# Queries and selection of the last twelve pairs as rows, turned into the score operand by one DMA transpose per head

## The chip, the cores and the metric

The kernel runs on one core of a Trainium2 chip. The metric is device microseconds of one execution; the figure for a kernel is the median of several runs. Work is done by TensorE (PE in the profile; PEld are its weight loads), VectorE (DVE), ScalarE (ACT) and GpSimd (POOL). SyncE (SP) computes nothing: it issues DMAs, in the order of its queue, and a DMA that has to wait for a semaphore holds up what stands behind it. Sixteen DMA engines serve all queues.

## The reference

The program is sparse attention followed by a feed-forward block. There are 4 batches, 8 heads, 768 positions and head dimension 64. Keys are cut into 24 chunks of 32. For each query an upper bound of the score is formed for every chunk from the chunk's smallest and largest key, and the 6 best causal chunks are kept:

```python
k_min, k_max = k_chunks.min(axis=3), k_chunks.max(axis=3)
ub = np.sum(np.maximum(q[:, :, :, None, :] * k_min[:, :, None, :, :], q[:, :, :, None, :] * k_max[:, :, None, :, :]), axis=-1)
ub = np.where(causal, ub, -1e9)
top_chunks = np.argsort(ub, axis=-1)[..., -6:]
scores = np.where(sel & causal_mask, scale * q @ k.T, -1e9)
attn = softmax(scores) @ v
```

The eight heads of a position are then one row of 512. Each row is divided by its root mean square and multiplied by a gain, and goes through `(silu(x @ w_gate) * (x @ w_val)) @ w_out` with a hidden width of 1536.

## The kernel before

**Pairs.** Two heads of one batch are a pair, since 2 x 64 dimensions fill 128 partitions. There are 16 pairs, 0 to 15, four for each batch, numbered in order of the batches.

**Preparation of a pair (`prep`).** The two heads' keys and queries are loaded in fp32 as rows, positions on partitions (`knat`, `qnat`; two DMAs each on SP's queue, line 479). TensorE turns them with six fp32 transposes each (line 498), and ScalarE or VectorE evicts them to `kt` and `qt`, dimensions on partitions. From `kt`, VectorE reduces the chunks' maxima and minima; from `qt` and its positive part `rt`, TensorE forms the bounds `ub` (line 586), which are turned back so that positions are on partitions (`up`), masked (`ubm`, line 618) and searched by twelve MAX8 instructions (line 631). `pick` (line 639 and 644) compares the bounds of both heads with their sixth best in one instruction and writes, beside the comparison, one column with a guard value from the best bound. Its destination is `selq`: 128 positions x 6 blocks x 2 heads x 64 columns.

**The score operands.** For each head of a pair there are two bf16 tiles of 128 partitions x 768 positions. `ke` holds 64 rows of keys and the rows of `e_all`, a constant with a large negative number where a key's chunk is. `qs` holds 64 rows of queries and the rows of the selection, so that one matmul gives the score and the penalty for chunks that aren't selected. Head 0 has the queries in partitions 0 to 63 and the selection in 64 to 127, head 1 the other way round. The query half is cast from `qt` (step qC: GpSimd, line 298; for pair 0 GpSimd or ScalarE). The selection half takes a step selT, six bf16 transposes of `selq` on TensorE into the PSUM tile `st` (line 655), and a step selC, two evictions `qs<-st` by ScalarE or VectorE. Three sets of operands exist, so three pairs can be in flight.

**Scores, product, norm.** `scores` computes key block by query block (`sc`, line 718), ScalarE exponentiates into `pt` (line 735), GpSimd masks the diagonal blocks for batches 1 to 3 (line 741), TensorE multiplies with the values `vx` (`av`, line 754; `vx` is loaded and cast by a DMA on GpSimd's queue, line 456), and VectorE divides into `xb`. `norm` scales the rows to `xs`; they are turned into `xT` by TensorE for batch 0 and by a DMA transpose on SP's queue for the others (line 842).

**Feed-forward.** `ffn` runs for each batch in two halves of 384 positions. For each of 12 hidden blocks four gate matmuls (`gp`, line 887), four value matmuls (`vp`, line 908), a tanh on ScalarE and two instructions on VectorE give a tile `hh`; three output tiles (`po`, line 928) follow, are evicted to `osb` and stored by SP (line 943).

**What sets the order.** Every piece of work is a step with a name, the engines that may do it, a cost for each, the buffers that it opens and uses, and a rank. `Order.run` goes through time with these costs; an engine that is free takes the ready step with the lowest rank. The ranks are sums of numbers in `RANK` (by kind of step, for batch 0 and for the others) and `TIMES` (by place: `a7` is the preparation of pair 7, `l7` its loads, `s7.0` its scores, `f2.1` a feed-forward half). The instructions are then issued in that order, fixed when the kernel is built, and each engine works its own queue in order. `SLOTS` gives the number of buffers of each kind. 88 dummy matmuls, `busy` (line 341), have ranks of 1000 and more: they fill TensorE where nothing else is ready; 48 may run at any time, 40 only after the scores of pair 2.

Of the kernel before, what the change touches and what calls it, by code (L numbers as in the profile page):

```python
# [24 lines left out]

RANK = (
    dict(
        av=144.2, dif=-491.58, eps=80.61, exp=-371.37, kC=299.85, kE=4.76, kT=-114.77,
        kload=9.63, kmn=30.2, kmx=-28.41, max=-225.53, qC=341.63, qE=-85.17, qT=-65.07,
        qload=37.04, relu=227.01, root=185.03, sc=127.33, sel=95.16, selC=107.08, selT=-124.54,  # L30
        sq=-359.31, tp=-102.27, tpE=5.42, ub=-213.91, ubE=-563.24, ubm=167.25, up=-358.34,
        vload=-60.34, xb=-160.93, xs=-122.34,
    ),
    dict(
        av=-11.76, dif=-2.19, eps=-312.61, exp=84.27, gate=-33.95, hh=-312.21, kC=-56.83,
        kE=197.29, kT=-62.54, kload=46.97, kmn=412.42, kmx=172.58, mask=54.76, max=242.91,
        out=-348.43, po=91.59, poE=382.1, qC=107.93, qE=-401.84, qT=31.34, qload=43.39,
        relu=98.28, root=-755.08, sc=-47.74, sel=57.49, selC=-254.04, selT=-245.0, sq=236.73,
        tanh=185.25, tg=-53.7, ub=-43.58, ubE=291.78, ubm=15.41, up=-21.92, val=-11.75,
        vload=304.71, xT=30.46, xb=28.85, xs=-150.44,  # L40
    ),
)

TIMES = {
# [15 lines left out]
}  # L60


# [139 lines left out]
def kernel(  # L202
# [82 lines left out]
    def pool(n):  # L285
        return 0.22 + n * 0.00085
# [23 lines left out]


    KU = [const.tile([P, 2, CH], FP32, name=f"ku{i}") for i in range(SLOTS["ku"])]
    SELQ = [const.tile([P, NT, 2, D], BF16, name=f"selq{i}") for i in range(SLOTS["selq"])]
    VX = [const.tile([P, 2 * NT, D + 1], BF16, name=f"vx{i}") for i in range(SLOTS["vext"])]
    e_all = const.tile([D, S], BF16, name="e_all")
# [28 lines left out]
    for i in range(BUSY):  # L344
# [3 lines left out]
            for i in range(SLOTS["ku"])]  # L348
    c_sel = [add("selq0", "DVE", 0.38, -90 + i, lambda e, i=i: nc.vector.memset(SELQ[i][:], 0.0))
             for i in range(SLOTS["selq"])]  # L350
# [28 lines left out]
    for i in range(NB):  # L379
        if i == 0:  # L380
            c_ke[i] = add("ke0", "", {"DVE": 1.05, "ACT": 1.4}, {"ke0": 1.0}, lambda e: (
                evict(e, KE[0][0][D:2 * D, :], e_all[:]),
                evict(e, KE[0][1][0:D, :], e_all[:])), [c_e])
        else:
            c_ke[i] = add("ke", "SP", 1.0, {"ke": 1.0}, lambda e, i=i: (
                nc.sync.dma_start(out=KE[i][0][D:2 * D, :], in_=e_all[:]),
                nc.sync.dma_start(out=KE[i][1][0:D, :], in_=e_all[:])), [c_e], load=180000)

    def make_cmf(n):
        if n == 0:  # L390
# [71 lines left out]
    def prep(c, i0, nb, at, lr):  # L462
# [3 lines left out]
        cols = slice(i0 * P, i0 * P + n)  # L466
        c0, c1 = i0 * 4, (i0 + nb) * 4
        nat, big = {}, {}
        done = {}
        for w, src in (("k", k), ("q", q)):  # L470
            nat[w], big[w] = Buf("nat"), Buf("qt")

# [10 lines left out]
            if p == 0:  # L483
                ld = [add(w + "load", "SP", 0.2, -200 + 2 * (w == "q") + r0 / 3,
                          lambda e, load=load, r0=r0: load(e, r0=r0, rn=3), opens=[nat[w]],
                          load=3 * P * 550) for r0 in range(0, nb, 3)]
            else:
                ld = [add(w + "load", "SP", 1.4, rank(lr, b, w + "load"), load, opens=[nat[w]],
                          load=n * 550)] * 2

            evs = []
            for j0 in range(0, nb, 3):
# [36 lines left out]
        reds = []  # L529
        step = 3 if p == 0 else nb  # L530
        for x0 in range(0, nb, step):
            after = done["k"][x0 // 3:(x0 + step) // 3]
            lead = {"": -10.0} if p == 0 and x0 == 0 else {}
            reds += [
                add("kmx", "DVE", 0.06 + step * P * 0.00106, {**rank(at, b, "kmx"), **lead},
                    lambda e, x0=x0: red(e, 0, x0, step), after, opens=[mx], uses=[big["k"]]),
                add("kmn", "DVE", 0.06 + step * P * 0.00106, {**rank(at, b, "kmn"), **lead},
                    lambda e, x0=x0: red(e, 1, x0, step), after + c_ku, opens=[c.ku],
                    uses=[big["k"]])]

        def diff(e):
            engine[e].tensor_tensor(
# [5 lines left out]
        c.dif[i0] = df  # L548


        casts = []
        for w, dst in (("k", KE), ("q", QS)):
            for hl in range(2):
# [71 lines left out]
        for j in range(0, nb, 3):  # L625
# [8 lines left out]
        sq = Buf("selq")  # L634

        def pick(e):
            s12 = SELQ[sq.slot][:, 0:nb].rearrange("p i h e -> p (i h) e")
            m12 = m8.tile[:, 0:nb].rearrange("p i h e -> p (i h) e")
            nc.vector.scalar_tensor_tensor(
                out=s12[:, :, 0:NCH],  # L640
                in0=m12[:, :, 5:6].to_broadcast([P, 2 * nb, NCH]),
                scalar=THRFLOOR, in1=ubm.tile[:, 0:nb].rearrange("p i h e -> p (i h) e"),
                op0=ALU.max, op1=ALU.is_gt)
            nc.vector.tensor_scalar(
                out=s12[:, :, NCH:NCH + 1], in0=m12[:, :, 0:1], scalar1=-GUARD,
                scalar2=0.0, op0=ALU.add, op1=ALU.max)
# [344 lines left out]
```

## Time and profile before

| | |
|---|---|
| median of 3 runs | 326.01 us (325.70 to 326.64) |
| the profiled execution's own time | 326.38 us |
| span from its first to its last instruction | 324.7 us |
| TensorE busy | 316.6 us, 2988 matmuls |
| VectorE, ScalarE, GpSimd busy | 248.0, 203.7, 117.8 us |
| DMA | 30.27 MB, mean 93 GB/s |

The profile gives, for one execution, the busy time of each engine, groups of instructions by source line and operands ("out<-in", with the count, the busy time, the mean of one, and the idle time of the engine just before them with what ended it), a chain of work followed back from the last instruction, and stretches of time with each engine's busy time. In a row of a chain the numbers are the start, the length and what ran. The DMA share is the mean busy share of the sixteen DMA engines; it can pass 1 where the records of packets overlap.

### The profile page before, as it was taken

How to read it: one execution, taken by the hardware profiler on the slowest of the kernel's cores; microseconds unless marked ns; L12 is line 12 of the kernel's file. 1: busy time of each engine (PE TensorE's matmuls, PEld its weight loads, DVE VectorE, ACT ScalarE, POOL GpSimd, SP SyncE). 2: the span in 40 equal slices, each digit the busy share in tenths (PEclk: the TensorE clock that was granted, in tenths of full speed). 3: DMA queues.
4: the chain of work that ended last, by engine and by line, in shares of the span. 5: the costliest groups of instructions: out<-in, count | busy, mean ns of one | idle time of the engine just before them, and what ended most of it. 6: DMA issues, size and time to landing. Idle time of an engine off the chain costs nothing.

```text
span 324.7 us, 7959 instructions
## 1 busy us (share of the span) xinstructions
PE 316.6 (98%) x2988; PEld 203.4 (63%) x3012; DVE 248.0 (76%) x668; ACT 203.7 (63%) x429; POOL 117.8 (36%) x171
## 2 busy tenths in 40 slices
PE   8998999999999999999999999999999999999995
PEld 4566777667577766765666667565666556556542
DVE  5788988898899989879978895666795978718320
ACT  4577989666459788994554799985339543333122
POOL 8658432435526766754000576842002200000000
PEclk9999999999999999999999999999999999999999
DMA  9999999998924499794000004454000260010022
GB/s 176 209 202 169 171 215 208 164 183 120 124 51 97 39 189 178 153 169 60 3 0 0 2 3 64 55 130 99 0 2 0 72 126 2 0 67 32 0 99 97
DMA packets 92503, 30.27 MB, mean 93 GB/s; under 512 B 85425, under 2 KB 89265, under 8 KB 92465
## 3 DMA queue, kind: packets, MB, share of 16 engines
q1 hardware_dynamic: 62352, 21.50, 28.8%
q0 software_dynamic: 28512, 7.87, 24.2%
q10 hardware_dynamic: 1600, 0.39, 0.6%
q8 instruction: 24, 0.39, 0.5%
q14 instruction: 15, 0.11, 0.1%
HBM read 28.57 MB, written 6.29 MB: 107 GB/s over the span
## 4 chain that ended last, share of the span: by engine, by line
PE 92%; DMA 3%; ACT 2%; DVE 1%; issue 1%; POOL 0%; ACTq 0%; POOLq 0%
PE vp L908 19%; PE gp L887 19%; PE po L928 19%; PE sc L718 10%; PE av L754 6%; PE ub L586 4%; PE busy L341 4%; PE pk L498 3%; PE pq L498 3%; DMA vx<-in_v_dram 3%; PE up L610 2%; PE st L655 1%; ACT pt L735 1%; PE sc L724 1%; PE tp L853 0%
## 5 line engine op out<-in xcount | busy, mean ns | idle before, releaser
L735 ACT ACTIVATE pt<-sc 128x512 bf16<-128x512 f32 (+3 forms) x192 | 90.1, 559 | 11.3 <-PE sc L718 8.4
L894 ACT ACTIVATE sg<-gp 128x384 bf16<-128x384 f32 x96 | 46.9, 492 | 59.2 <-PE gp L887 58.4
L908 PE MATMUL vp<-xT,wv 128*128 128x384 bf16 x384 | 77.0, 326 | 0.4 <-ACT xT L294 0.4
L887 PE MATMUL gp<-xT,wg 128*128 128x384 bf16 x384 | 75.5, 326 | 0.0
L900 DVE SCALAR_TENSOR_TENSOR tg<-sg,gp 128x384 bf16<-128x384 bf16 x96 | 52.1, 551 | 25.2 <-ACT sg L894 23.1
L928 PE MATMUL po<-wo,hh 128*128 128x512 bf16 x268 | 66.7, 379 | 1.1
L916 DVE TENSOR_TENSOR hh<-vp,tg 128x384 bf16<-128x384 f32 x96 | 52.5, 552 | 10.8 <-PE vp L908 9.0
L718 PE MATMUL sc<-qs,ke 128*128 128x128 bf16 (+4 forms) x417 | 55.3, 250 | 0.0
L887 PEld LDWEIGHTS <-wg 128*128 128x128 bf16 x384 | 36.9, 98 | 24.8 <-issue 0.8
L908 PEld LDWEIGHTS <-wv 128*128 128x128 bf16 x384 | 36.6, 98 | 24.2 <-issue 1.5
L741 POOL TENSOR_SCALAR_AFFINE_SELECT pt<-pt 128x512 bf16<-128x512 bf16 (+1 forms) x48 | 26.2, 563 | 57.0 <-ACT pt L735 56.6
L298 POOL CAST qs<-qt 64x768 bf16<-64x768 f32 x30 | 27.3, 911 | 45.2 <-ACT qt L294 34.4
L928 PEld LDWEIGHTS <-hh 128*128 128x128 bf16 x288 | 26.7, 98 | 25.2
L754 PE MATMUL av<-vx,pt 128*128 128x65 bf16 x672 | 41.0, 194 | 1.2 <-DMA vx<-in_v_dram 1.0
L754 PEld LDWEIGHTS <-pt 128*128 128x128 bf16 x672 | 33.6, 98 | 12.3 <-DMA vx<-in_v_dram 1.5
L718 PEld LDWEIGHTS <-ke 89*128 89x128 bf16 (+1 forms) x420 | 30.0, 97 | 8.5 <-issue 1.6
L298 POOL CAST ke<-kt 64x768 bf16<-64x768 f32 x31 | 27.0, 870 | 15.2 <-ACT kt L294 10.9
L294 ACT ACTIVATE qs<-st 64x768 bf16<-64x768 bf16 x26 | 20.9, 805 | 5.9 <-PE st L655 5.5
L296 ACT ACTIVATE osb<-po 128x512 f32<-128x512 f32 x19 | 11.5, 605 | 20.7 <-PE po L928 20.6
L341 PE MATMUL busy<-zeros 128*128 128x512 bf16 (+1 forms) x87 | 20.9, 358 | 1.3 <-DVE zeros L336 1.3
L775 DVE TENSOR_TENSOR xb<-av,rden 128x384 bf16<-128x384 f32 (+1 forms) x34 | 18.2, 534 | 1.2
L631 DVE MAX8 m<-ubm 128x8 f32<-128x24 f32 x192 | 18.7, 168 | 0.2
(72 smaller groups left out, 339.8 us busy)
## 6 DMA issues: line engine op xcount, KB each, us to landing
out_dram<-osb SPq DMA_DIRECT2D x24, 256.0 KB, 2.1
knat<-in_k_dram SPq DMA_DIRECT2D x30, 192.0 KB, 4.4
qnat<-in_q_dram SPq DMA_DIRECT2D x30, 192.0 KB, 4.7
vx<-in_v_dram POOLq DMA_DIRECT2D x16, 192.0 KB, 5.3
wv<-in_moe_w_val_dram POOLq DMA_DIRECT2D x2, 768.0 KB, 10.2
wg<-in_moe_w_gate_dram POOLq DMA_DIRECT2D x2, 768.0 KB, 9.6
wo<-in_moe_w_out_dram POOLq DMA_DIRECT2D x2, 768.0 KB, 10.4
ke<-e_all SPq DMA_DIRECT2D x4, 96.0 KB, 3.6
```

The source lines that it names most:

```text
L298: engine[e].tensor_copy(out_, in_)
L341: nc.tensor.matmul(t[:, 0:n], zeros[:, 0:P], zeros[:, 0:n], start=True, stop=True)
L718: nc.tensor.matmul(t[:, x:x + m, :].rearrange("p a b -> p (a b)"), ke[kk, kb * P:(kb + 1) * P], qs[kk, q0 * P:(q0 + m) * P], start=not tri ...
L735: nc.scalar.activation(out=t[:, 0:nn, :], in_=sc.tile[:, 0:nn, :], func=ACT.Exp, scale=SCALE)
L741: nc.gpsimd.affine_select(out=pt.tile[:, 0:nd, :], in_=pt.tile[:, 0:nd, :], compare_op=ALU.is_ge, fill=0.0, base=0, pattern=[[0, nd], [1, ...
L754: nc.tensor.matmul(av.tile[:, qi - i0, :], pt.tile[:, x, :], VX[c.v.slot][:, hl * NT + kb, :], start=(begin and m == 0), stop=(left[0] == ...
L887: nc.tensor.matmul(t[:], wg[:, g, hs], XT[b].tile[:, g, cols], start=(g == 0), stop=(g == NP - 1))
L894: nc.scalar.activation(out=t[:], in_=gp.tile[:], func=ACT.Tanh, scale=0.5)
L900: nc.vector.scalar_tensor_tensor(out=t[:], in0=sg.tile[:], scalar=1.0, in1=gp.tile[:], op0=ALU.add, op1=ALU.mult)
L908: nc.tensor.matmul(t[:], wv[:, g, hs], XT[b].tile[:, g, cols], start=(g == 0), stop=(g == NP - 1))
L916: nc.vector.tensor_tensor(out=t[:], in0=vp.tile[:], in1=tg.tile[:], op=ALU.mult)
L928: nc.tensor.matmul(po.tile[:], hhs[ht].tile[:, th * P:(th + 1) * P], wo[:, ht, :], start=(ht == 0), stop=(ht == NHT - 1))
```

## The change

For pairs 4 to 15 the query half and the selection half of `qs` are no longer made separately. A new buffer `qn` (two of them, 128 x 1792 bf16, cleared once) holds for each position and head 128 columns: 64 of the query and 64 of the selection, in the order in which the head's `qs` has them as partitions. A new step qN copies the loaded queries into it, casting to bf16, on GpSimd or VectorE. `pick` writes the comparison and the guard there, one head at a time. Two steps qX, one for each head, issue a DMA transpose of 128 x 768 on SP's queue, from `qn` into the whole of `qs`. The steps qC, selT and selC are gone for these pairs; the turned queries `qt` are still made, for the bounds. To make room, `nat` goes from 8 to 7 buffers, `selq` from 3 to 2 and `hh` from 36 to 33. The diff also has a path for keys as rows, which `ROWS=16` leaves unused (no pair reaches it, and `kb=0` makes no buffer). All numbers in `RANK` and `TIMES` are replaced, so that the order of all steps is another.

```diff
 RANK = (
-        av=144.2, dif=-491.58, eps=80.61, exp=-371.37, kC=299.85, kE=4.76, kT=-114.77,
+        av=132.14, dif=-438.04, eps=7.54, exp=-319.11, kC=334.22, kE=136.01, kT=-485.02,
...
 TIMES = {
...
+    ROWS, QM, SEL2 = 16, 4, 0.42
+    QC, HW = S // (CH // 4), NT * P + D
...
-    SLOTS = dict(ps=8, nat=8, vext=4, set=3, ku=3, selq=3, qt=7, ubs=2, small=8, ubm=3,
-                 pt=10, xb=2, xt=2, row=3, xs=4, ff=8, hh=36, ob=3)
+    SLOTS = dict(ps=8, nat=7, kh=1, km=1, kb=0, qn=2, vext=4, set=3, ku=3, selq=2, qt=7, ubs=2, small=8, ubm=3,
+                 pt=10, xb=2, xt=2, row=3, xs=4, ff=8, hh=33, ob=3)
...
+    QN = [const.tile([P, 2 * HW + P], BF16, name=f"qn{i}") for i in range(SLOTS["qn"])]
...
+    c_qn = [add("qn0", "DVE", 0.5, {"qn0": 1.0}, lambda e, i=i: nc.vector.memset(QN[i][:], 0.0))
+            for i in range(SLOTS["qn"])]
...
+        rows_k, side_q = p >= ROWS, p >= QM
...
+        def lay(e, buf, bases, w):
+            evict(e, bases[buf.slot][:, 0:2 * (HW + D)].rearrange("p (h t d) -> p h t d", h=2, d=P)
+                  [:, :, 0:NT, 0:D], nat[w].tile[:].rearrange("p t h d -> p h t d"))
+
+        def turned(bases, buf, dst, name, deps):
+            def move(e, hl):
+                nc.sync.dma_start_transpose(
+                    out=dst[c.set.slot][hl][:].rearrange("d (t p) -> d t p", p=P),
+                    in_=bases[buf.slot][:, hl * HW:hl * HW + NT * P])
+
+            return [add(name, "SP", 1.4, rank(at, b, name, hl, "step"), lambda e, hl=hl: move(e, hl),
+                        deps, opens=[c.set], uses=[buf], load=240000) for hl in range(2)]
...
         for w, dst in (("k", KE), ("q", QS)):
+            if rows_k if w == "k" else side_q:
+                continue
             for hl in range(2):
...
+        if side_q:
+            qn = Buf("qn")
+            qs_n = add("qN", "", {"POOL": pool(n), "DVE": 0.5}, rank(at, b, "qN"),
+                       lambda e: lay(e, qn, QN, "q"), ready["q"][:1] + c_qn, opens=[qn],
+                       uses=[nat["q"]], port=True)
...
         def pick(e):
+            if side_q:
+                for y in range(2):
+                    s12 = QN[qn.slot][:, D:D + 2 * NT * P].rearrange(
+                        "p (h t d) -> p h t d", h=2, d=P)[:, 1 - y]
+                    nc.vector.scalar_tensor_tensor(
+                        out=s12[:, :, 0:NCH], in0=m8.tile[:, :, y, 5:6].to_broadcast([P, NT, NCH]),
+                        scalar=THRFLOOR, in1=ubm.tile[:, :, y], op0=ALU.max, op1=ALU.is_gt)
+                    nc.vector.tensor_scalar(
+                        out=s12[:, :, NCH:NCH + 1], in0=m8.tile[:, :, y, 0:1], scalar1=-GUARD,
+                        scalar2=0.0, op0=ALU.add, op1=ALU.max)
+                return
...
-        pk = add("sel", "DVE", 0.18 + nb * 48 * 0.00104, rank(at, b, "sel"), pick, [last] + c_sel,
-                 opens=[sq], uses=[m8, ubm], port=True)
+        pk = add("sel", "DVE", (SEL2 if side_q else 0.18) + nb * 48 * 0.00104, rank(at, b, "sel"), pick,
+                 [last] + (c_qn if side_q else c_sel), opens=[qn if side_q else sq], uses=[m8, ubm],
+                 port=True)
+        if side_q:
+            c.sel = turned(QN, qn, QS, "qX", [pk, qs_n])
+            return c.sel
```

More of the change, by code (lines that the diff above doesn't have):

```diff
@@ L27 @@
     dict(
-        av=144.2, dif=-491.58, eps=80.61, exp=-371.37, kC=299.85, kE=4.76, kT=-114.77,
[L29 to L32, printed above, removed]
+        av=132.14, dif=-438.04, eps=7.54, exp=-319.11, kC=334.22, kE=136.01, kT=-485.02,
+        kload=-54.57, kmn=-137.23, kmx=-301.52, max=-152.41, qC=109.54, qE=316.44, qT=171.34,
+        qload=-51.07, relu=59.75, root=77.15, sc=154.73, sel=83.19, selC=291.06, selT=-117.97,
+        sq=-378.33, tp=24.59, tpE=360.56, ub=-188.41, ubE=-631.05, ubm=-71.86, up=-402.33,
+        vload=-29.64, xb=-262.2, xs=247.58,
     ),
     dict(
[L35 to L40, printed above, removed]
+        av=-265.86, dif=4.6, eps=-792.39, exp=258.27, gate=4.29, hh=-241.0, kC=134.04,
+        kE=332.01, kT=-79.45, kload=194.09, kmn=455.81, kmx=359.92, mask=48.28, max=274.06,
+        out=-113.88, po=207.1, poE=221.55, qE=-270.87, qN=298.48, qT=-27.26, qX=-362.48,
+        qload=199.51, relu=279.63, root=-878.4, sc=-37.49, sel=336.13, sq=111.91, tanh=315.81,
+        tg=61.58, ub=88.65, ubE=-137.69, ubm=107.32, up=172.52, val=34.42, vload=256.19,
+        xT=-70.38, xb=-239.74, xs=-343.95,
     ),
@@ L312 @@
     KU = [const.tile([P, 2, CH], FP32, name=f"ku{i}") for i in range(SLOTS["ku"])]
+    KB = [const.tile([P, 2 * HW + P], BF16, name=f"kb{i}") for i in range(SLOTS["kb"])]
+    QN = [const.tile([P, 2 * HW + P], BF16, name=f"qn{i}") for i in range(SLOTS["qn"])]
     SELQ = [const.tile([P, NT, 2, D], BF16, name=f"selq{i}") for i in range(SLOTS["selq"])]
@@ L387, with turn_e, copy_e @@
                 nc.sync.dma_start(out=KE[i][1][0:D, :], in_=e_all[:])), [c_e], load=180000)
+    c_kb = []
+    if ROWS < B * NP:
+        et = Buf("ps", "prep")
+        def turn_e(e):
+            t = tile_of(et, [P, NT, D], BF16, "et")
+            for j in range(NT):
+                nc.tensor.transpose(t[:, j], e_all[:, j * P:(j + 1) * P], ident_b[0:D, 0:D])
+        def copy_e(e):
+            for x in KB:
+                evict(e, x[:, D:D + 2 * NT * P].rearrange("p (h t d) -> p h t d", h=2, d=P)
+                      [:, :, :, 0:D], et.tile[:].rearrange("p (o t) d -> p o t d", o=1).to_broadcast(
+                          [P, 2, NT, D]))
+        c_et = add("eT", "PE", 0.2, {"eT": 1.0}, turn_e, [c_e, c_idb], opens=[et])
+        c_kb = [add("eC", "", {"DVE": 2 * 0.5, "ACT": 2 * 0.75}, {"eT": 1.0}, copy_e, [c_et], uses=[et])]
     def make_cmf(n):
@@ L468, in prep @@
         nat, big = {}, {}
-        done = {}
+        done, ready = {}, {}
+        rows_k, side_q = p >= ROWS, p >= QM
         for w, src in (("k", k), ("q", q)):
@@ L489, in prep @@
                           load=n * 550)] * 2
+            ready[w] = ld
+            if w == "k" and rows_k:
+                continue
             evs = []
@@ L527, in red @@
                                         axis=AXX, op=ALU.min)
[L529 to L539, printed above, removed]
+        def lay(e, buf, bases, w):
+            evict(e, bases[buf.slot][:, 0:2 * (HW + D)].rearrange("p (h t d) -> p h t d", h=2, d=P)
+                  [:, :, 0:NT, 0:D], nat[w].tile[:].rearrange("p t h d -> p h t d"))
@@ new lines, in prep, with load_h, whole, turn_m @@
+        if rows_k:
+            kh, km, kt = Buf("kh"), Buf("km"), Buf("ps", "prep")
+            def load_h(e):
+                t = tile_of(kh, [QC, 2, CH // 4, D], FP32, "khalf")
+                for h in range(2):
+                    nc.sync.dma_start(out=t[:, h], in_=k[b, h0 + h].rearrange(
+                        "(c t) d -> c t d", t=CH // 4))
+            ldh = add("khload", "SP", 1.4, rank(lr, b, "khload"), load_h, opens=[kh], load=220000)
+            def whole(e, which):
+                op = ALU.min if which else ALU.max
+                if not which:
+                    tile_of(km, [QC, 2, CH // 8, D], FP32, "kmm")
+                to, src = (kh if which else km).tile, kh.tile
+                m = CH // 8
+                while m:
+                    nc.vector.tensor_tensor(out=to[:, :, 0:m], in0=src[:, :, 0:m],
+                                            in1=src[:, :, m:2 * m], op=op)
+                    src, m = to, m // 2
+            w_x = add("kmx", "DVE", 1.15, rank(at, b, "kmx"), lambda e: whole(e, 0), [ldh], opens=[km],
+                      uses=[kh])
+            w_n = add("kmn", "DVE", 1.15, rank(at, b, "kmn"), lambda e: whole(e, 1), [w_x], uses=[kh])
+            def turn_m(e):
+                t = tile_of(kt, [P, 2, QC], FP32, "kmt")
+                for m, x in ((0, km), (1, kh)):
+                    nc.tensor.transpose(t[:, m], x.tile[:, :, 0, :], ident_f[0:QC, 0:QC])
+            tmt = add("kT", "PE", 0.19, rank(at, b, "kT"), turn_m, [w_x, w_n, c_id], opens=[kt],
+                      uses=[km, kh])
+            def join(e):
+                tile_of(mx, [P, NCH], FP32, "kmx")
+                for m in range(2):
+                    nc.vector.tensor_reduce(
+                        out=KU[c.ku.slot][:, 0, 0:NCH] if m else mx.tile[:],
+                        in_=kt.tile[:, m].rearrange("p (c t) -> p c t", t=4),
+                        axis=AXX, op=ALU.min if m else ALU.max)
+            reds.append(add("join", "DVE", 0.44, rank(at, b, "join"), join, [tmt] + c_ku,
+                            opens=[mx, c.ku], uses=[kt]))
+            kb = Buf("kb")
+            kn = add("kN", "", {"POOL": pool(n), "DVE": 0.5}, rank(at, b, "kN"),
+                     lambda e: lay(e, kb, KB, "k"), ready["k"][:1] + c_kb, opens=[kb], uses=[nat["k"]],
+                     port=True)
+            casts += turned(KB, kb, KE, "kX", [kn])
+        else:
+            step = 3 if p == 0 else nb
+            for x0 in range(0, nb, step):
+                after = done["k"][x0 // 3:(x0 + step) // 3]
+                lead = {"": -10.0} if p == 0 and x0 == 0 else {}
+                reds += [
+                    add("kmx", "DVE", 0.06 + step * P * 0.00106, {**rank(at, b, "kmx"), **lead},
+                        lambda e, x0=x0: red(e, 0, x0, step), after, opens=[mx], uses=[big["k"]]),
+                    add("kmn", "DVE", 0.06 + step * P * 0.00106, {**rank(at, b, "kmn"), **lead},
+                        lambda e, x0=x0: red(e, 1, x0, step), after + c_ku, opens=[c.ku],
+                        uses=[big["k"]])]
@@ L633, in prep @@
             last = add("max", "DVE", 0.52, rank(at, b, "max", j, "step"), top, [last], opens=[m8], uses=[ubm])
-        sq = Buf("selq")
+        sq = None if side_q else Buf("selq")
         def pick(e):
+            if side_q:
[9 more added lines that the diff above has]
+                return
             s12 = SELQ[sq.slot][:, 0:nb].rearrange("p i h e -> p (i h) e")
```

4 lines of the change are left out of this document (3 added, 1 removed), and 30 rows, old and new, of the table TIMES.

## The prediction

> **What bounds the kernel now.** I read the page first, then the same span cut into stretches, then the chain of work that ended last, then the rows of the operands that the change touches.
>
> ```profile
> span 324.7 us, 7959 instructions
> PE 316.6 (98%) x2988; PEld 203.4 (63%) x3012; DVE 248.0 (76%) x668; ACT 203.7 (63%) x429; POOL 117.8 (36%) x171
> PE 92%; DMA 3%; ACT 2%; DVE 1%; issue 1%; POOL 0%; ACTq 0%; POOLq 0%
> ```
>
> TensorE is busy for 98% of the span and carries 92% of the chain. VectorE is next with 76%. The stretches tell where that holds (span and busy us with instruction counts for PE, PEld, DVE, ACT and POOL, then granted clock, DMA share, GB/s):
>
> ```profile
> 0.00:56.00 56.00, 52.98 (x632) 37.30 (x635) 45.69 (x151) 41.18 (x84) 31.24 (x51) 1.00 1.17 193
> 56.00:290.00 234.00, 232.93 (x2197) 150.26 (x2216) 190.46 (x494) 153.47 (x329) 86.57 (x120) 1.00 0.45 75
> 290.00:324.70 34.70, 30.64 (x163) 15.86 (x162) 11.89 (x23) 9.09 (x17) 0.00 (x0) 1.00 0.15 54
> ```
>
> From 56 to 290 us TensorE is idle for 234.00 - 232.93 = 1.1 us. In the prelude it is idle for 56.00 - 52.98 = 3.0 us, and it also does filler there: the dummy matmuls "busy", which run when nothing else is ready. At the end it stops about 4 us before the last store. A busy share can hide slack, since ends of matmuls are modelled, so I checked the rate on the chain (start, us, what):
>
> ```profile
> 41.42 0.34 PE st L655 x6
> 52.63 0.33 PE st L655 x6
> 56.46 3.90 PE gp L887 x24
> 281.88 5.99 PE po L928 x27
> 313.67 7.08 PE po L928 x32
> ```
>
> 24 gate matmuls of 384 columns start 3.90 / 24 = 0.163 us apart, and output matmuls of 512 columns 5.99 / 27 = 0.222 us and 7.08 / 32 = 0.221 us apart: 0.42 to 0.43 ns per column in both shapes, at a granted clock of 1.00. They follow one another without a pause. So after 56 us each us of TensorE work is a us of time, as long as the order keeps TensorE fed. That is the rule of the sum.
>
> The Trainium skill (Perfetto Trace Analysis, "Identifying the Most-Contended Engine") warns that matmul busy share is a poor measure of headroom and names the weight loads' share instead. Here that share is 63%, and by it taking matmuls away need gain nothing; the rows above, spaced by their column counts, disagree with that reading for this kernel.
>
> **The change part by part.**
>
> *The selection's transpose on TensorE goes.* Each pair turns its selection with six transposes (line 655). The busy time of the operand st on TensorE, by stretch (length, busy us, count, clock, DMA share, GB/s):
>
> ```profile
> 0.00:56.00 56.00, 2.51 (x30) 1.00 1.17 193
> 56.00:100.00 44.00, 0.50 (x6) 1.00 0.89 130
> 100.00:150.00 50.00, 1.99 (x24) 1.00 0.80 133
> 150.00:200.00 50.00, 1.99 (x24) 1.00 0.14 15
> 200.00:252.00 52.00, 1.00 (x12) 1.00 0.22 46
> ```
>
> 30 of the 96 lie before 56 us: pairs 0 to 4. The change touches pairs 4 to 15, so one of its twelve pairs is in the prelude, where TensorE has filler to do, and eleven are in the saturated stretch (6 + 24 + 24 + 12 = 66). Six take 0.34 us of the chain (the rows at 41.42 and 52.63 above); the 0.50 us of busy time for six counts the overlap of pipelined ends. So the term is 11 x 0.34 = 3.7 us, bounded by 0 (if something else ends the stretch) and 12 x 0.50 = 6.0 us.
>
> *Evictions and casts go, one layout copy comes.*
>
> ```profile
> L298 POOL CAST qs<-qt 64x768 bf16<-64x768 f32 x30 | 27.3, 911 | 45.2 <-ACT qt L294 34.4 <-DVE qt L298 9.3 <-DVE ku L542 0.7
> L294 ACT ACTIVATE qs<-st 64x768 bf16<-64x768 bf16 x26 | 20.9, 805 | 5.9 <-PE st L655 5.5
> L568 DVE TENSOR_SCALAR rt<-qt 128x768 f32<-128x768 f32 x16 | 11.8, 738 | 0.3
> L639 DVE SCALAR_TENSOR_TENSOR selq<-m,ubm 128x288 bf16<-128x288 f32 x16 | 8.2, 511 | 0.1
> L644 DVE TENSOR_SCALAR selq<-m 128x12 bf16<-128x12 f32 x16 | 6.6, 412 | 0.0
> L349 DVE MEMSET selq<- 128x384 uint32 x3 | 1.1, 378 | 0.1
> ```
>
> ScalarE and VectorE lose 24 evictions qs<-st (about 24 x 0.805 = 19 us, nearly all ScalarE's). GpSimd loses 24 casts, 24 x 0.911 = 21.9 us, and gains at most twelve copies of the queries into rows. Such a copy has 768 columns as the cast has, on twice the partitions: taken at 0.91 us on GpSimd, 10.9 us, or 0.74 on VectorE by the row of line 568. None of this is on the chain after 56 us, so I cost it at nothing either way; the cover is TensorE's own queue of feed-forward matmuls.
>
> *VectorE's selection is split by head.* Two compares and two guards per pair instead of one each, at half width. The extra price is bounded by nothing but a fixed part below (about 0.2 us, a guard's shortest case being nearly all fixed) and a whole second pair above (0.51 + 0.41 = 0.92 us). I take 0.25, nearer to the guard: 12 x 0.25 = 3 us, up to 11. If VectorE took all layout copies as well, that is 12 x 0.74 = 8.9 more. VectorE has 234.00 - 190.46 = 43.5 us free in the saturated stretch, but less where preparation is dense:
>
> ```profile
> 75.00:100.00 25.00, 24.95 (x254) 17.14 (x255) 22.98 (x68) 14.93 (x33) 11.48 (x14) 1.00 0.83 108
> 100.00:125.00 25.00, 24.73 (x341) 17.70 (x345) 23.34 (x68) 19.54 (x43) 18.60 (x27) 1.00 0.68 120
> 125.00:150.00 25.00, 24.79 (x259) 16.28 (x262) 21.64 (x51) 22.40 (x53) 16.85 (x23) 1.00 0.92 146
> ```
>
> There it has 75 - 67.96 = 7.0 us, and pairs 5 to 9 bring 5 x 0.25 = 1.3 us (5 x 0.99 = 5.0 us with the copies): it fits. Clearing the new row buffers once (two of 1792 columns against one of 768 less) costs 2 x 0.378 x 1792 / 768 - 0.378 = 1.4 us of VectorE in the prelude, where it has 56.00 - 45.69 = 10.3 us free.
>
> *Two DMA transposes per pair come, on SP's queue.* The nearest rows are the kernel's own transposes of the scaled rows (xT, 128 x 512; issue ns min/median/max, then landing counted from the start of the issue), five of them in a row, a stretch in which almost only they run, and SP's longest waits:
>
> ```profile
> L842 SPq DMA_TRANSPOSE xT<-xs x18: 1194/1218/2152, 130.9 to 264.9; - x18
> DMA to landing us min/median/max: 2.4/2.5/5.1
> 212.89 6.44 SPq L842 DMA_TRANSPOSE xT<-xs x5
> 214.00:219.00 5.00, 4.95 (x43) 2.99 (x43) 3.12 (x6) 3.89 (x9) 2.48 (x3) 1.00 0.52 105
> SPq L943 <- ACT osb L296: 77.2, 16, 20.6
> SPq L943 <- DVE osb L300: 54.3, 3, 52.3
> ```
>
> A transpose of 128 x 768 is bounded by 1.2 us of issue (all fixed) and 1.5 x 1.22 = 1.8 us (all by size); I take 1.8, since the work is 1.5 times as much. 24 of them hold SP for 44 us at most. SP stands waiting for output tiles alone for 77.2 + 54.3 = 131 us, so as a queue it has room. Of the 16 DMA engines, 0.52 x 5.00 = 2.6 us served about 5.00 / (6.44 / 5) = 3.9 issues, 0.67 us each; times 1.5, times 24: 24 us, while the share in the saturated stretch is 0.45 of 234 us. Room again.
>
> *The path from selection to scores gets longer.* Pair 5 before (start, us, what):
>
> ```profile
> 93.06 0.18 DVE L644 TENSOR_SCALAR selq<-m 128x12 bf16<-128x12 f32 x1
> 93.64 0.50 PE L655 MATMUL st<-ident_b,selq 128*128 128x128 bf16 x6
> 94.18 1.63 ACT L294 ACTIVATE qs<-st 64x768 bf16<-64x768 bf16 x2 [0.49 <-PE st L655]
> 96.12 1.04 PE L718 MATMUL sc<-qs,ke 89*128 89x128 bf16 x10
> ```
>
> From the end of the guard (93.24) to the first score matmul is 2.9 us. After: issue 1.8 plus the landing's 2.5 - 1.2 = 1.3, so 3.1 us for the first head and 4.9 for the second; at the longest landing (5.1 - 2.5 = 2.6 more) 5.7 and 7.5. The first head is about where it was, the second 2 us later. The new wait is on SP: behind a transpose that waits for the selection or for a free operand set stand the k and q loads, the output stores and the xT transposes; an output store held up there would hold an output tile, then ScalarE's eviction, then a PSUM bank. I cost this at nothing: between score matmuls TensorE has gate, value and output matmuls of another batch, and 2 us is three gate groups. The cover ends if the written order has put the scores where the data isn't there yet.
>
> *The rest.* One load buffer, three hidden-row buffers and one selection buffer fewer: a feed-forward half uses 12 hidden buffers, so 33 still hold both halves of a batch (24). All rank numbers of the planner change, so the whole order is another one. Nothing in this trace prices that: below, it can save the prelude's idle 3.0 us; above, it can lose some. I take zero.
>
> **Sum.** -3.7 us on TensorE after 56 us; everything else hidden. The profiled execution took 326.38 us, 0.4 over the median of 326.01; it becomes 322.7, and the median 326.0 - 3.7 = 322.3 us.
>
> **The rivals.**
>
> *Shorter still.* The relief of ScalarE and GpSimd and another order also close TensorE's idle 3.0 us in the prelude: 322.3 - 3.0 = 319.3. For it: 31.24 of 56 us of GpSimd there, and pair 4's casts and evictions are gone from it. Against it: the filler's count stays, and pairs 0 to 3, which set the prelude, keep the old path.
>
> *No gain.* TensorE's busy row hides slack, or the saved 0.34 us are taken again by VectorE, which is 92% busy between 75 and 125 us. Then 326.0. Against it stand the spacing of the matmuls and the 43.5 us that VectorE has free. The skill's rule on busy share, cited above, points to this rival.
>
> *Slower: the transposes land late.* Place: the first score matmuls of pairs 5 to 9, between 75 and 150 us, where k, q and v loads keep the DMA share at 0.68 to 0.92 and a landing can take 5.1 instead of 2.5 us. TensorE runs in order; if its queue reaches the scores before the landing, it stands. It decides from 3.7 / 12 = 0.3 us of standing per pair. At half of the 2.6 us for five pairs, both heads, it costs 5 x 2 x 1.3 = 13 us at most, half of that if the second head hides behind the first: 322.3 + 6.5 = 328.8. For it: in the trace before, scores follow the selection at once (96.12 after 95.81). Against it: xT went the same way under load without a stall of TensorE longer than those 1.1 us in all.
> The Trainium skill (VectorE: DVE Perf Modes, "The three transpose paths") gives 390 ns for a 128 x 128 bf16 transpose on TensorE and 1309 ns by DMA, and prefers TensorE. An estimate from that page would be 6 x 1.309 = 7.9 us per head; the trace disagrees, with four such tiles landing in 2.5 us.
>
> **How the numbers follow.** 322.3 has a chance of 0.55, with a range of its own from 320.5 to 324.5; shorter still 0.12; no gain 0.13; late landings 0.20. So faster by over 0.3% (1.0 us, about what a measurement of this kernel can tell from no change) 0.67, within it 0.13, slower 0.20. The range reaches from 319.0, just under the second case, to 328.5, just under the last one's time.
>
> **What would show it.** Right: 24 transposes qs<-qn issued on SP in 1.8 us each, landing 3 to 4 us after the issue began; 24 st transposes left on TensorE; about 19 us less of evictions and 11 us less on GpSimd; TensorE's idle from 56 us on no more than 2 us. Wrong: waits of TensorE on DMA qs in the chain between 75 and 150 us; SP waiting on the selection while TensorE or ScalarE waits for a load or a store; a first gate matmul well after 55 us, from the new order; or VectorE appearing in the chain.

## The result

The changed kernel takes 320.15 us in the median of six runs (320.09 to 320.69), beside 325.41 us for the kernel before. The ratio is 0.9841, with a 95% interval of 0.9818 to 0.9863: 5.2 us less, 4.5 to 5.9. Forecast were 322.3 us (3.7 us less), a range of 319.0 to 328.5, and 0.67 for faster. Where some executions of a kernel fell into a slower state of the chip, its figure below is the median of the others.

**The profile after.** Its span is 319.0 us, 5.7 less; the profiled execution took 320.69 us. The page's first and fourth part, then the three stretches in the columns of the prediction:

```profile
span 319.0 us, 7874 instructions
PE 312.6 (98%) x2922; PEld 199.6 (63%) x2940; DVE 237.2 (74%) x684; ACT 189.7 (59%) x418; POOL 105.1 (33%) x155
PE 96%; DVE 2%; issue 1%; ACT 0%; ACTq 0%; DVEq 0%
```

```profile
0.00:56.00 56.00, 54.44 (x658) 38.65 (x661) 44.90 (x140) 42.45 (x91) 35.27 (x55) 1.00 1.08 168
56.00:290.00 234.00, 233.24 (x2143) 148.84 (x2156) 186.12 (x534) 140.47 (x315) 69.85 (x101) 1.00 0.64 100
290.00:319.00 29.00, 24.93 (x125) 12.13 (x125) 6.14 (x12) 6.74 (x12) 0.00 (x0) 0.98 0.20 73
```

TensorE is busy for 4.0 us less (316.6 to 312.6) and idle for 1.7 us less (324.7 - 316.6 = 8.1 before, 319.0 - 312.6 = 6.4 after); the two are the whole difference of the spans. The idle time went mostly in the prelude: 56.00 - 54.44 = 1.6 us where it had been 3.0. TensorE's waits, first of the kernel before, then of the changed one (who waited, for whom, us in total, times, longest):

```profile
PE busy L341 <- DVE zeros L336: 1.3, 1, 1.3
PE av L754 <- DMA vx<-in_v_dram: 1.0, 1, 1.0
PE vp L908 <- ACT xT L294: 0.4, 1, 0.4
```

```profile
PE busy L345 <- DVE zeros L340: 1.3, 1, 1.3
```

The wait for the values' load (1.0 us) and the one for batch 0's turned rows (0.4 us) are gone. The new operand's rows in the changed kernel (ns min/median/max, first and last start) and the landing of its transposes:

```profile
L739 DVE SCALAR_TENSOR_TENSOR qn<-m,ubm x24: 289/300/314, 78.8 to 214.1; 128x144 bf16<-128x144 f32 x24
L742 DVE TENSOR_SCALAR qn<-m x24: 172/174/385, 79.0 to 214.3; 128x6 bf16<-128x6 f32 x24
L563 SPq DMA_TRANSPOSE qs<-qn x24: 1210/1236/1971, 79.7 to 221.8; - x24
L300 POOL CAST qn<-qnat x8: 812/822/1132, 29.5 to 212.0; 128x768 bf16<-128x768 f32 x8
L300 DVE CAST qn<-qnat x4: 551/551/552, 95.9 to 138.7; 128x768 bf16<-128x768 f32 x4
DMA to landing us min/median/max: 2.5/2.7/5.3
```

A transpose of 128 x 768 holds SP for 1.24 us, no longer than one of 128 x 512, and lands after 2.7 us. Even so it isn't the next thing before the scores. For pair 5 (start, us, what):

```profile
89.93 0.17 DVE L742 TENSOR_SCALAR qn<-m 128x6 bf16<-128x6 f32 x1
90.25 2.54 SPq L563 DMA_TRANSPOSE qs<-qn  x2
102.71 0.67 PE L831 MATMUL sc<-qs,ke 128*128 128x128 bf16 x9
```

Its first score matmul is the second of these nine (the first one belongs to pair 4) and starts at 102.8, 12.7 us after the selection ended; before, that was 2.9 us. In the changed kernel's trace the first operand of each of the twelve pairs landed between 2.8 us (pair 13) and 14.9 us (pair 12) before the weight load of its first score matmul. The new order makes the selection that much earlier than it needs to be.

Part of ScalarE's relief was spent on VectorE. ScalarE evicts 24 of the turned key tiles where it had evicted 16. VectorE's busy time fell by 10.8 us (248.0 to 237.2), and the eight key tiles that it no longer evicts are 4.5 us of that (8.7 to 4.2):

```profile
L294 ACT ACTIVATE kt<-pk 128x384 f32<-128x384 f32 x16 | 7.6, 490 | 4.9 <-PE pk L498 4.6 <-ACT pt L735 0.2
```

```profile
L296 ACT ACTIVATE kt<-pk 128x384 f32<-128x384 f32 x24 | 11.2, 499 | 3.2 <-PE pk L526 2.4 <-PE av L867 0.3 <-issue 0.2
```

### The profile page after: what moved, and what is told of

It is laid out like the page before. It is cut to its first block, busy times and chain, and to the rows that moved or that the text cites. A ratio compares the mean times of both kernels' runs of the same rounds, so it can differ in the third digit from the quotient of the medians.

```text
span 319.0 us, 7874 instructions
## 1 busy us (share of the span) xinstructions
PE 312.6 (98%) x2922; PEld 199.6 (63%) x2940; DVE 237.2 (74%) x684; ACT 189.7 (59%) x418; POOL 105.1 (33%) x155
## 4 chain that ended last, share of the span: by engine, by line
PE 96%; DVE 2%; issue 1%; ACT 0%; ACTq 0%; DVEq 0%
PE vp L1021 20%; PE gp L1000 20%; PE po L1041 19%; PE sc L831 11%; PE av L867 6%; PE ub L684 5%; PE busy L345 5%; PE pk L526 4%; PE pq L526 3%; PE up L708 2%; PE sc L837 1%; PE st L768 0%; PE tp L966 0%; DVE kmx L552 0%; DVE qs L300 0%
## 5 line engine op out<-in xcount | busy, mean ns | idle before, releaser
L1021 PE MATMUL vp<-xT,wv 128*128 128x384 bf16 x384 | 75.8, 326 | 0.1
L831 PE MATMUL sc<-qs,ke 89*128 89x128 bf16 (+5 forms) x420 | 53.3, 251 | 0.1
L1041 PEld LDWEIGHTS <-hh 128*128 128x128 bf16 x288 | 27.5, 98 | 28.5 <-issue 0.4
L854 POOL TENSOR_SCALAR_AFFINE_SELECT pt<-pt 128x512 bf16<-128x512 bf16 (+1 forms) x48 | 25.4, 544 | 55.2 <-ACT pt L848 55.1
L867 PEld LDWEIGHTS <-pt 128*128 128x128 bf16 x672 | 31.4, 98 | 10.7 <-issue 2.1
L867 PE MATMUL av<-vx,pt 128*128 128x65 bf16 x672 | 36.7, 194 | 0.0
L300 POOL CAST ke<-kt 64x768 bf16<-64x768 f32 x31 | 27.7, 895 | 14.3 <-ACT kt L296 8.1
L298 ACT ACTIVATE osb<-po 128x512 f32<-128x512 f32 x21 | 12.7, 605 | 29.3 <-PE po L1041 29.2
L944 DVE SCALAR_TENSOR_TENSOR xs<-xb,ri,gains 128x512 bf16<-128x512 bf16 x24 | 17.6, 766 | 1.7 <-DMA xT<-xs 1.7
L633 POOL TENSOR_TENSOR ku<-kmx,ku 128x24 f32<-128x24 f32 x9 | 3.2, 357 | 45.4 <-DVE ku L554 42.8
(77 smaller groups left out, 322.3 us busy)
```

The lines of the kernel that those rows point to most:

```text
L300: engine[e].tensor_copy(out_, in_)
L831: nc.tensor.matmul(t[:, x:x + m, :].rearrange("p a b -> p (a b)"), ke[kk, kb * P:(kb + 1) * P], qs[kk, q0 * P:(q0 + m) * P], start=not tri ...
L854: nc.gpsimd.affine_select(out=pt.tile[:, 0:nd, :], in_=pt.tile[:, 0:nd, :], compare_op=ALU.is_ge, fill=0.0, base=0, pattern=[[0, nd], [1, ...
L867: nc.tensor.matmul(av.tile[:, qi - i0, :], pt.tile[:, x, :], VX[c.v.slot][:, hl * NT + kb, :], start=(begin and m == 0), stop=(left[0] == ...
L1021: nc.tensor.matmul(t[:], wv[:, g, hs], XT[b].tile[:, g, cols], start=(g == 0), stop=(g == NP - 1))
L1041: nc.tensor.matmul(po.tile[:], hhs[ht].tile[:, th * P:(th + 1) * P], wo[:, ht, :], start=(ht == 0), stop=(ht == NHT - 1))
```

## The experiments

The theory: after the prelude TensorE's work is the time, so the 72 transposes taken away are worth 72 x 0.056 = 4.0 us, and the rest came from the prelude's waits. The rivals: the relief of ScalarE and GpSimd gained; the order alone gained; and, for the margin, that late operands are near to stopping TensorE. Every ratio is to the kernel before, run on the same chip.

**TensorE's work put back.** The changed kernel's order, with six dummy matmuls in each pair from 4 on:

```diff
             t = tile_of(up, [P, G, nj, 2, CH], FP32, "up")
+            for _ in range(6 if side_q else 0):
+                nc.tensor.matmul(t[:].rearrange("p g j h c -> p (g j h c)")[:, 0:P], zeros[:, 0:P],
+                                 ident_b[:], start=True, stop=True)
```

> The changed kernel with its order untouched, and before the bounds are turned back in each of pairs 4 to 15 six throw-away matmuls of 128 columns on TensorE, as many as the change took away; nothing reads them. Theory (TensorE's work is the time): 12 x 0.336 = 4.0 us slower than the changed kernel, 320.2 + 4.0 = 324.2 us, still about 1.2 us under the kernel before. Rival (the gain came from the evictions and casts taken off ScalarE and GpSimd, and TensorE's busy row hides slack): no difference, 320.2 us.

Measured: 324.64 us, ratio 0.9964 (0.9949 to 0.9979). Against 0.9841 that is 0.0123 x 325.4 = 4.0 us slower, as the theory has it, and not the rival's nothing (the two intervals together leave some 3.1 to 4.9; against a later measurement of the changed kernel, 0.9857, it is 3.5). With TensorE's work back, the new order and the relief of the other engines are still 1.2 us faster than the kernel before, 0.7 to 1.7. The span grew by 3.6 us and TensorE's busy time by 3.4, for these instructions:

```profile
L707 PE MATMUL up<-ident_b,zeros 128*128 128x128 bf16 x72 | 6.0, 219 | 0.0
```

**TensorE's work taken away in the old order.**

```diff
-            for j in range(nb):
+            for j in range(nb if p < 4 else 1):
                 nc.tensor.transpose(
...
-                evict(e, QS[c.set.slot][hl][rows, cols], st.tile[rows, :])
+                if p < 4:
+                    evict(e, QS[c.set.slot][hl][rows, cols], st.tile[rows, :])
+                else:
+                    evict(e, QS[c.set.slot][hl][rows, cols].rearrange("p (o q) -> p o q", q=P),
+                          st.tile[rows, 0:P].rearrange("p (o q) -> p o q", o=1).to_broadcast(
+                              [D, NT, P]))
```

> The kernel before with its order untouched, but in pairs 4 to 15 only one of the six transposes of the selection is made, and the evictions read that one block six times; so the selection of five blocks in six is left out, and evictions, casts and DMAs stay as they were. Theory: 12 x 5 x 0.056 = 3.4 us less than the kernel before, 325.4 - 3.4 = 322.0 us. Rival (slack on TensorE): 325.4 us.

Measured: 323.57 us, ratio 0.9936 (0.9912 to 0.9960): 2.1 us less, 1.3 to 2.9. Neither theory nor rival: work that leaves TensorE gains time in the old order too, but about 60% of its length, and the expected 3.4 lies outside the interval. Why the rest is missing, this run doesn't show.

**Six pairs, with the old numbers.** The changed program with the numbers of the kernel before (and ranks for the new steps), `QM=10`:

```diff
-    ROWS, QM, SEL2 = 16, 4, 0.42
+    ROWS, QM, SEL2 = 16, 10, 0.42
-    SLOTS = dict(ps=8, nat=7, kh=1, km=1, kb=0, qn=2, vext=4, set=3, ku=3, selq=2, qt=7, ubs=2, small=8, ubm=3,
-                 pt=10, xb=2, xt=2, row=3, xs=4, ff=8, hh=33, ob=3)
+    SLOTS = dict(ps=8, nat=8, kh=1, km=1, kb=0, qn=2, vext=4, set=3, ku=3, selq=3, qt=7, ubs=2, small=8, ubm=3,
+                 pt=10, xb=2, xt=2, row=3, xs=4, ff=8, hh=27, ob=3)
```

> The change for the last six pairs alone (10 to 15), with the rank numbers of the kernel before, three selection buffers, eight load buffers and 27 hidden-row buffers; TensorE's order is that of the kernel before until well past the prelude. Theory: 6 x 0.336 = 2.0 us less than the kernel before, 323.4 us, with the prelude's waits as they were. Rival (the new order is what gained): 325.4 us or more.

Measured: 324.65 us, ratio 0.9970 (0.9952 to 0.9988): 1.0 us less, 0.4 to 1.6. So the path gains without the new numbers, and half of what its TensorE work is worth. From 200 to 250 us TensorE is idle for 1.2 us where it was 0.3 in the kernel before, and its new waits in this trace say where some of that went; with the old ranks one operand lands only when its scores are due:

```profile
PE sc L831 <- DMA qs<-qn: 0.6, 1, 0.6
PE av L867 <- ACT pt L848: 0.4, 1, 0.4
```

**The prelude's wait for values.** In the kernel before, the first two loads of values exchange places:

```diff
     done = order.run(PLACE)
+    loads = [s for s in done if s.name == "v"]
+    loads[0].emit, loads[1].emit = loads[1].emit, loads[0].emit
```

> The kernel before, with the first two loads of values exchanged, so that those which TensorE needs first are the first to be loaded; all else, and every engine's order, as before. Theory (the part of the gain beyond TensorE's work is waits in the prelude, 1.0 us of them for these values): 1.0 us less than the kernel before, 324.4 us. Rival (the prelude is set by VectorE's chain, and TensorE's wait there is covered later): 325.4 us.

Measured: 325.25 us, ratio 0.9987 (0.9970 to 1.0004). The wait of 1.0 us is gone from the trace, and the time moved by 0.4 us with nothing in the interval, whose other end is the 1.0 us of the theory. So neither theory nor rival is out: whether this wait is a part of the 1.2 us by which the gain exceeds TensorE's work can't be told.

**Later operands.** In the changed kernel, a throw-away transpose of the same rows goes ahead of each of the 24, then two:

```diff
             def move(e, hl):
+                for y in range(1):
+                    nc.sync.dma_start_transpose(
+                        out=SELQ[(hl + y) % 2][:].rearrange("d t h p -> d t (h p)"),
+                        in_=bases[buf.slot][:, hl * HW:hl * HW + NT * P])
                 nc.sync.dma_start_transpose(
```

> The changed kernel with its order untouched, and one throw-away DMA transpose of the same rows ahead of each of the 24, into a selection buffer that nothing reads any more: the first head's operand lands some 1.3 us later, the second's 2.6 us, and SP is held 24 x 1.24 = 30 us longer. Theory (other matmuls cover the longer path): within 0.5 us of 320.2 us. Rival (late landings stop TensorE): 12 x 1.3 = 16 us to 12 x 2.6 = 31 us more, 336 to 351 us.

> As the run with one throw-away transpose ahead of each, but with two: operands land some 2.6 and 5.2 us later and more, since transposes into the same buffer wait for one another. It looks for where the cover ends. Theory: the cover is a few gate groups, so some pairs begin to cost, 1 to 10 us over the changed kernel. Rival: twice the loss of the other run.

Measured: 334.95 us with one (ratio 1.0295, 1.0253 to 1.0337), 14.8 us over the changed kernel, and 366.82 us with two (1.1273, 1.1226 to 1.1320), 47 us over and more than three times the loss with one. So the theory that other work covers a longer path fell. But the rival's reason is not what the trace with one shows:

```profile
PE pk L526 <- DMA knat<-in_k_dram: 2.9, 1, 2.9
PE av L871 <- POOL pt L858: 2.6, 1, 2.6
PE pq L526 <- DMA qnat<-in_q_dram: 2.1, 2, 1.6
PE sc L835 <- DMA qs<-qn: 0.2, 1, 0.2
```

Score matmuls waited for the operand once, for 0.2 us. TensorE waited for keys and queries of later pairs, whose loads stand behind the transposes on SP, and for masks.

**SP held, operands in time.** The same number of throw-away transposes, but behind each pair's two and reading a weight tile:

```diff
                     in_=bases[buf.slot][:, hl * HW:hl * HW + NT * P])
+                for y in range(2 * hl):
+                    nc.sync.dma_start_transpose(
+                        out=SELQ[y][:].rearrange("d t h p -> d t (h p)"), in_=wg[:, 0, 0:S])
```

> The changed kernel with its order untouched, and the 24 throw-away DMA transposes of the run late_one put behind each pair's own two instead of ahead of them, and reading a weight tile instead of the rows: SP is held as long, but the pair's operands and row buffers are not late by their own throw-away transposes. Theory from the trace of late_one, where operands still landed ahead of every score matmul (loads behind them on SP came late, and GpSimd waited for row buffers): loads alone, half of late_one's loss, 5 to 9 us over the changed kernel. Rival (landing of the operands): within 1 us of 320.2 us.

Measured: 332.47 us, ratio 1.0231 (1.0200 to 1.0262). The changed kernel, run again beside it, took 320.50 us with 0.9857 (0.9838 to 0.9875), so this is 0.0374 x 325.0 = 12.2 us over: most of late_one's loss, more than expected, and the rival is out. SP's queue in the changed kernel, then in this one, then what TensorE met:

```profile
98.50 2.65 SPq L563 DMA_TRANSPOSE qs<-qn  x2
102.83 1.11 SPq L504 DMA_DIRECT2D knat<-in_k_dram  x2
```

```profile
98.64 4.49 SPq L563 DMA_TRANSPOSE qs<-qn  x2
103.17 2.62 SPq L567 DMA_TRANSPOSE selq<-wg  x2
106.73 1.10 SPq L504 DMA_DIRECT2D knat<-in_k_dram  x2
```

```profile
113.05 0.87 PE L526 MATMUL pk<-ident_f,knat 128*128 128x128 f32 x3 [5.26 <-DMA knat<-in_k_dram]
```

A key load issued 3.9 us later stops TensorE for 5.3 us, with its queue full of work behind that one transpose of keys. The issue isn't all of it: the second half of this load landed 3.7 us after its issue in the changed kernel and 5.7 us after it here. So the 12.2 us are the price of the added transposes as SP's time and as traffic together; no run tells the two apart.

**One more transpose moved to the DMA.** In the changed kernel's order, batch 0's second half is turned by DMA as the other batches are:

```diff
             def turn(e, xs=xs, tp=tp):
+                if half:
+                    return
...
+                if half:
+                    nc.sync.dma_start_transpose(out=XT[b].tile[:, :, i * P:(i + 1) * P], in_=xs.tile[:])
+                    return
                 evict(e, XT[b].tile[:, :, i * P:(i + 1) * P], tp.tile[:])
```

> The changed kernel with its order untouched, where the second half of batch 0 is turned by three DMA transposes on SP, as the other batches are, in place of twelve transposes on TensorE and three evictions. Theory: 12 x 0.056 = 0.7 us less if a cover is there, 319.5 us; but its rows are turned at 69.5 to 71.5 us and may be needed at once, and then the longer way costs 2 us, 322 us.

> The changed kernel once more, beside the other three on the same chip: 320.2 us.

Measured: 330.24 us, ratio 1.0154 (1.0134 to 1.0175), 9.7 us over the changed kernel; both expectations missed. The three transposes are issued from 64 us on, while weights and values load; the landing of these three, the DMA share (last but one of the columns) between 56 and 78 us, and TensorE's wait:

```profile
DMA to landing us min/median/max: 8.8/10.2/11.6
56.00:78.00 22.00, 14.68 (x115) 9.18 (x112) 16.67 (x53) 7.92 (x17) 7.63 (x9) 0.89 1.16 166
PE gp L1005 <- DMA xT<-xs: 8.4, 1, 8.4
```

This is the late-landing rival as it was meant, at another place: beside these weight and value loads a transpose landed after 10 us, not after 2.7. The change's own first transposes are issued at 79.7 us, near the end of that load, and landed after 5.0 us at most before 100 us. The DMA share alone doesn't tell the two cases apart: between 100 and 150 us in the changed kernel it is 1.08 to 1.11, and there the longest landing was 5.3 us. Which of the loads made the difference isn't shown.

This stop also cost more than its length. The granted clock is 0.50 from 73.2 to 83.4 us, while TensorE stands from 70.7 to 79.1; the page's row has it in tenths (9 is 0.9 or more), 40 slices to the span, and below it is what ran first afterwards:

```profile
PEclk9999999995999999999999999999999999999999
79.13 2.72 PE L1005 MATMUL gp<-xT,wg 128*128 128x384 bf16 x8 [8.45 <-DMA xT<-xs]
```

These gate matmuls are 2.72 / 8 = 0.34 us apart, twice the 0.163 at a clock of 1.00. With 4.3 us of work at half the clock, some 2.1 us lost, the estimate is 8.4 + 2.1 - 0.7 = 9.8 us for the 9.7 measured. In the run with SP held the clock is 0.50 from 111.3 to 118.1 us and from 142.0 to 145.4, behind stops of 5.3 and 2.0 us: another 4 us of its 12.2, by the same estimate. In the run with one throw-away transpose ahead of each, the clock falls in the same way (112.6 to 119.4 and 184.3 to 187.7).

**ScalarE's and GpSimd's work put back.** The changed kernel's order, with two throw-away copies on ScalarE and two casts on GpSimd at each pair's selection, then each alone:

```diff
             if side_q:
+                for y in range(2):
+                    nc.scalar.activation(out=SELQ[0][0:D].rearrange("p t h d -> p (t h d)"), in_=e_all[:],
+                                         func=ACT.Copy)
+                    nc.gpsimd.tensor_copy(
+                        SELQ[1][0:D].rearrange("p t h d -> p (t h d)").rearrange("p (o n) -> p o n", o=3),
+                        gains[0:D, 0:256].rearrange("p (o n) -> p o n", o=1).to_broadcast([D, 3, 256]))
```

> The changed kernel with its order untouched, and with each pair's selection (pairs 4 to 15) two throw-away copies of 64 x 768 on ScalarE and two throw-away casts of 64 x 768 on GpSimd, as many as the change took away; nothing reads them, and TensorE's work stays as the change left it. Theory (TensorE's work gained, the relief of ScalarE and GpSimd gains nothing by itself): within 1 us of 320.2 us. Rival (the relief is part of the gain): some 1.5 us or more over it, up to all of the 5.2.

> As the run evictions_back, but with the two throw-away copies on ScalarE alone. It is to tell which engine's relief counts. If ScalarE's: most of that run's 8.4 us, since the exponentials wait in ScalarE's queue and TensorE's products wait for them. If GpSimd's: under 2 us over the changed kernel.

> As the run evictions_back, but with the two throw-away casts on GpSimd alone. If GpSimd's relief counts (the masks of the diagonal blocks wait in its queue, and TensorE's products wait for them): most of the 8.4 us. If ScalarE's: under 2 us over the changed kernel.

Measured: both 328.94 us, ratio 1.0120 (1.0102 to 1.0139); ScalarE alone 328.78 us, 1.0101 (1.0078 to 1.0124); GpSimd alone 322.38 us, 0.9907 (0.9886 to 0.9929). Over the changed kernel that is some 8.4, 8 and 2 us. So in the new order 24 copies on ScalarE are not free, and cost more than the whole gain. With ScalarE's alone, the copies and then the stretch from 56 to 290 us and TensorE's waits:

```profile
L737 ACT ACTIVATE selq<-e_all x24: 829/842/859, 78.1 to 222.5; 64x768 bf16<-64x768 bf16 x24
56.00:290.00 234.00, 226.54 (x2104) 143.64 (x2102) 182.31 (x525) 154.90 (x334) 69.96 (x100) 1.00 0.65 98
PE av L870 <- ACT pt L851: 2.6, 4, 1.3
PE av L870 <- POOL pt L857: 2.4, 3, 1.3
```

24 x 0.84 = 20.2 us of ScalarE's time make TensorE idle for 234.00 - 226.54 = 7.5 us there, 6.7 more than the 0.8 of the changed kernel. The exponentials stand in ScalarE's queue behind the copies, the masks wait for the exponentials, and the products for both. That the old kernel paid 8 us for its evictions doesn't follow: its order was laid around them. Nor do the copies put back exactly the old load: ScalarE had done 22 of the 24 evictions, it now also does the eight key tiles, and with the copies it is busy for 206.6 us, where it was 203.7 before the change.

## Why the prediction was right, and where it wasn't

*TensorE is the bound, and its matmuls without a pause are the time: right in the new order.* 72 dummy matmuls cost 4.0 us at a weight-load share of 63%. The rival without gain is out. So is, for this kernel, the reading beside it that the weight loads' share of 63% leaves room (the Trainium skill, Perfetto Trace Analysis, "Identifying the Most-Contended Engine"; the page also names the share of peak FLOP/s, which was not worked out here). The term of 3.7 us for eleven pairs can't be told from 4.0 for twelve. The number itself did less well than the mechanism: 320.15 us lies just under the main case's own range (320.5 to 324.5) and nearer to "shorter still" (319.3) than to 322.3.

*"None of this is on the chain after 56 us, so I cost it at nothing either way": the reason failed for ScalarE, the sum hardly did.* An engine's relief was priced by its absence from the chain, but an eviction in an in-order queue delays the exponential behind it. In the new order 20.2 us of copies on ScalarE cost 8 us and casts on GpSimd cost 2, so that order needs the relief. What the relief and the order gained together, beside TensorE's work, is the 1.2 us that are left with this work put back; the relief alone, in the old order, was not run.

*"The cover ends if the written order has put the scores where the data isn't there yet": the condition was right, the cover named was not.* The three gate groups weren't what covered the path: in the new order the operands are there 3 to 15 us early. With the old numbers six pairs gain half of their work's length.

*The new wait on SP, costed at nothing: right, with little to spare.* The queue has 131 us of waiting for output tiles, as computed, but that is not where the key loads stand; 30 us more on it cost 12 to 15, the half-clock stretches included. What breaks first is what was named as standing behind a transpose, the loads, not the score operand.

*Sizes.* Issue 1.24 us, not 1.8: fixed, not by size. Landing 2.7 us from the start of the issue, where 3.1 was taken; the bound of 5.1 held for the change's own transposes but for 0.2 us (5.3), and was too low beside the weight loads, where 10.2 was measured. Selection on VectorE: 2 x (0.30 + 0.17) = 0.94 us a pair against the median of 0.45 + 0.19 before, 0.30 more, where 0.25 was taken. By the means that the prediction read, which a few long instructions raise, there is next to no difference (0.92 before). TensorE's idle time from 56 us on is 0.8 us, under the 2 named.

*The remaining 1.2 us.* 5.2 measured less 4.0 for TensorE's work; the new order was priced at zero. The profile puts 1.4 us in the prelude, between the forecast and the rival "shorter still"; the one wait of it that was taken away in the old kernel gave no time that could be told from none. That 320.15 us still lies in the forecast range is owed to the width left for another case, not to the sum. It stays open how this part divides between the prelude and the order after it.

## What to carry to other kernels

Where one engine runs without a pause, work taken off it is worth its spacing (not its busy time), provided that the order written for the others keeps it fed; put the same path into the old order and half may be lost. Price a new DMA by what stands behind it on its issuing queue and by the load of the DMA engines at that moment, not by its landing time in a quiet stretch. Engines that are off the chain of the profile may be so because the order was laid around their work: putting work on their queues is not free. And count a long stop of TensorE at more than its length when the trace shows a lower granted clock behind it.

## What the runs showed of the hardware

A DMA transpose holds SP for 1.24 us with 128 x 768 as with 128 x 512 (1.22), so larger ones are cheaper by the tile. Its landing went from 2.5 us in a quiet stretch to 8.8 to 11.6 us beside weight and value loads at a DMA share of 1.16, though others landed within 5.3 us at a share of 1.1. A key load issued 3.9 us late stopped TensorE, with other work queued behind the one transpose, for 5.3 us. And behind stops of TensorE of 8.4, 5.3, 2.9, 2.6 and 2.0 us it worked for some us at a granted clock of 0.50; gate matmuls behind the first of these started 0.34 us apart instead of 0.163. In the run with copies on ScalarE, whose longest stop was 1.3 us, the clock stayed at 1.00.
